# A chunked state-space scan ahead of a gated FFN: every chunk scanned as two halves of 64 tokens on the two halves of the partitions

## The chip, the cores and the metric

The kernel runs on one core of a Trainium2 chip. The metric is the device time of one execution in microseconds, as the median of several runs. A core has five engines that work side by side, each through its own list of instructions in a fixed order: PE (TensorE, matrix products), DVE (VectorE), ACT (ScalarE), POOL (GpSimd) and SP (SyncE, which here only issues DMAs). They wait for one another by semaphores.

## The reference

For each of 4 batches and 8 heads, a sequence of 768 tokens is run through a linear scan with a state of 16 x 32, written in chunks; the result, laid out as 3072 tokens by 256 features, goes through a gated FFN of width 1536. Cut to what matters:

```
for c in range(nc):                                   # chunks of the sequence
    la = log_a[:, :, sl];  cum = np.cumsum(la, axis=-1)
    L = np.exp(cum[..., :, None] - cum[..., None, :]) * causal
    M = np.einsum('bhin,bhjn->bhij', Cc, Bc) * L      # C by B, weighed by decays
    y_intra = np.einsum('bhij,bhjd->bhid', M, xc)     # the product within the chunk
    y_inter = np.einsum('bhin,bhnd->bhid', Cc, state) * np.exp(cum)[..., None]   # the state product
    y[:, :, sl] = y_intra + y_inter
    Bx = np.einsum('bhjn,bhjd->bhjnd', Bc, xc) * decay_from_j[..., None, None]
    state = decay_full[..., None, None] * state + np.sum(Bx, axis=2)
x = y.transpose(0, 2, 1, 3).reshape(batch * seq, heads * head_dim)
out = (sigmoid(x @ w_gate) * (x @ w_val)) @ w_out
```

The length of a chunk is free: any split of the sequence gives the same result.

## The kernel before

The sequence is cut into six chunks of 128 tokens (`L = 128`, `NCH = 6`). One chunk of one batch, with its eight heads, is a *unit*; there are 24, numbered u = 4c + b. The FFN runs once per chunk over the 512 tokens of its four units: 12 blocks f of `gate` and `value` (lines 725 to 766), then four projections `proj` (line 810). Chunk 0's FFN takes plain fp32 weights (line 795, 827); from chunk 1 on, weights and inputs are split in a high and a low fp32r part (lines 804, 837, 838). The split of the weights (`split_w`, `part_w`, lines 305 to 341) runs on ACT, DVE and POOL during chunk 0's FFN and into chunk 1's.

A unit of chunks 1 to 5 does this (class `Unit`, line 357; tile names in brackets as in the profile):

- `products`: B and C are transposed on PE (`pt`, lines 383, 384); ACT copies them and makes two masked copies of C, one for each half of the heads (`bct`, lines 394 to 400).
- `multiply` (line 499): C by B for all tokens of the chunk, four matmuls of 32 rows by 128 columns by 256 (`pcb`, line 506), into four PSUM banks that two units share.
- `decays` (line 412): the decays a are loaded from DRAM (`a_z`), spread over all 128 partitions, and one DVE scan over 8 x 128 elements turns them into all decay products (`ab`, line 418); B is multiplied by the decay to the end of the chunk (line 424).
- `before` (line 429): C times the decay from the start of the chunk (`cd`, line 434), from prefix products loaded from DRAM (`a_p`, tile `pp`).
- `result` (chunk 1, line 436) and `results` (chunks 2 to 5, two units at once, line 516): DVE weighs C by B by the decays (`m`, lines 440 and 524, 8 x 128 columns). Then PE makes the state product, two matmuls of 128 x 128 x 128 with the state masked into a block matrix (`sb`; lines 457 and 536), and into the same bank the product within the chunk, eight matmuls of 128 rows by 32 columns by 144 (lines 463 and 544). The last 16 of the 144 columns give the unit's part of the new state. Then ACT and DVE take the output into the FFN's high and low inputs (`xh`, `xl`), and DVE transposes the state part (lines 480 and 564).
- `state` (line 482): DVE adds the decayed old state (line 486), POOL or DVE makes the block matrix from it (line 494).

Chunk 0 (class `FirstUnit`, line 566) already works in two halves of 64 tokens, the first on partitions 0 to 63 and the second on 64 to 127. Its decays are spread on PE (`pa`, line 585), C by B is made of 32 x 64 tiles (line 605), the product within of 64 x 32 tiles with 80 columns (line 647), the second half's state product from the first half's transposed state (lines 655, 659). There C is permuted on PE (`pc`, line 615), since heads lie in another order on the state's rows.

The order of every engine's list is set ahead by a planner in Python (`run`, line 175). Each piece of work is a task with a due time (`DUES` and `task`, lines 18 and 164) whose steps name an engine, an assumed cost, the keys that must be made before, and the PSUM banks or buffers that they take (`banks` for three general ones, `cb` for the C by B group). The planner always takes the next step that could begin, by due time. SP's DMAs are steps in the same plan; the first nineteen loads have a written order (`FIRST`, line 31).

Of the kernel before, what the change touches and what calls it, by code (L numbers as in the profile page):

```python
# [8 lines left out]
F32 = mybir.dt.float32  # L9
# [31 lines left out]
GV0 = 1.75  # L41
# [22 lines left out]
def tile_ssd_then_gated_ffn(  # L64
# [22 lines left out]
    LB = L + N  # L87
# [3 lines left out]
    NBUF = 3  # L91

    const = ctx.enter_context(tc.tile_pool(name="const", bufs=1))
    ld = ctx.enter_context(tc.tile_pool(name="ld", bufs=NBUF))
# [3 lines left out]
    ps_mm = ctx.enter_context(tc.tile_pool(name="ps_mm", bufs=3, space=PSUM))  # L98
    ps_cb = ctx.enter_context(tc.tile_pool(name="ps_cb", bufs=1, space=PSUM))
    ps_y = ctx.enter_context(tc.tile_pool(name="ps_y", bufs=1, space=PSUM))  # L100
# [12 lines left out]
    for i in range(WARM):  # L113
# [17 lines left out]
    delta2 = hp.tile([P, H, L2], F32, tag="h3", name="delta2")  # L131
    nc.gpsimd.tensor_copy(delta2, eye2.rearrange("p (o l) -> p o l", o=1).broadcast_to([P, H, L2]))
# [13 lines left out]
        of_row.rearrange("p (q g n) -> p q g n", q=NQ, g=NG),  # L146
        head.rearrange("p (g q o) -> p q g o", g=NG, o=1).broadcast_to([NB * H, NQ, NG, N]),
    )

    perm = hp.tile([P, P], F32, tag="h6", name="perm")  # L150
    nc.gpsimd.tensor_copy(
        perm.rearrange("p (q g n) -> p q g n", q=NQ, g=NG), eye.rearrange("p (g q n) -> p q g n", g=NG, q=NQ)
    )
    delta = const.tile([P, H, L], F32, name="delta")
    st = [const.tile([P, D], F32, name=f"st{b}") for b in range(NB)]

    sb = [const.tile([P, NG, NQ, D], F32, name=f"sb{b}") for b in range(NB)]
# [17 lines left out]
    def run():  # L175
# [8 lines left out]
        spare = {"banks": [0.0] * 3, "cb": [0.0], "g": [0.0] * 3, "o": [0.0] * 2}  # L184
# [68 lines left out]
    def load_bc(c, b, n):  # L253
        cs = slice(c * L, (c + 1) * L)
        for tag, src in (("bn", b4), ("cn", c4)):
            t = pair_of(tag, c, b, N)
            if c == 0:
                nc.sync.dma_start(  # L258
                    t[:, b % 2 : b % 2 + n].rearrange("p b h n -> p (b h) n"), src[cs, b * H : (b + n) * H]
                )  # L260
                continue
            for i in range(b, b + n):
                for g in range(NG):
                    nc.sync.dma_start(  # L264
                        t[:, i % 2].rearrange("p (q g) n -> g p q n", g=NG)[g],
                        src[cs, i * H + NQ * g : i * H + NQ * (g + 1)],
                    )
# [6 lines left out]
    def load_a(c, b):  # L274
        u = c * NB + b
        t = ld.tile([P, H, L], F32, tag="ab", name=f"ab{c}_{b}", bufs=NBUF + 1)
        nc.sync.dma_start(t, a_z[b : b + 1, :, c * L : (c + 1) * L].broadcast_to([P, H, L]))
        got["a", u] = t

    def load_p(c, b):  # L280
        t = ld.tile([P, L], F32, tag="pp", name=f"pp{c}_{b}")
# [73 lines left out]
    units = {}  # L355

    class Unit:


        def __init__(self, c, b):  # L360
            self.c, self.b, self.u = c, b, c * NB + b
            self.nm = f"{c}_{b}"
            self.more = c < NCH - 1
            self.w = LB if self.more else L
            self.m = None

        def second(self):

            if self.m is None:
                self.m = wk.tile([P, H, LB], F32, tag="m", name=f"m{self.nm}")  # L370
            return self.m

        def products(self):
# [3 lines left out]
            if c:  # L377
                needs += [("bct", u - 1 if c > 1 else -1), ("cb", u - 2), ("cd", u - 2)]
            needs += [("x", 0, NB - 1)] if c == 1 else []
            yield step("pe", 0.24 if c else 0.45, needs, [("tp", u)], banks=1)  # L380
            bn, cn = (got[k, c, b // 2][:, b % 2].rearrange("p h n -> p (h n)") for k in ("bn", "cn"))
            pt = ps_mm.tile([P, 512], F32, tag="mm", name=f"pt{self.nm}")
            nc.tensor.transpose(pt[:, :L], bn, eye)
            nc.tensor.transpose(pt[:, L : 2 * L], cn, eye)
            yield step("act", 0.9 if c else 1.1, [], [("bct", u)], banks=-1)
            if c:
                self.bct = wk.tile([P, 4, L], F32, tag="bct", name=f"bct{self.nm}")
# [14 lines left out]
            if c == 0:  # L402
                yield step("pe", 0.47, [], [("cb", u)])
                self.multiply()
            elif u == NB:
                yield step("pe", 0.85, [("mult", v) for v in range(NB)], [("cb", u)], cb=1)
                self.multiply()

        def multiply(self):
            multiply(self)  # L410

        def decays(self):

            c, b, u = self.c, self.b, self.u
            yield step("dve", 2.3, [("a", u), ("delta",)], [("scan", u)], port=True)
# [6 lines left out]
            if self.more:  # L422
                yield step("dve", 0.28, [("bc", u), ("scan", u), ("y", u - 2)], [("bdec", u)], port=True)
                nc.vector.tensor_tensor(
                    out=self.second()[:, :, L:], in0=got["bn", c, b // 2][:, b % 2],
                    in1=self.dec[:, :, L - 1 : L].broadcast_to([P, H, N]), op=ALU.mult,
                )

        def before(self):

            c, b, u = self.c, self.b, self.u
            yield step("dve", 0.42, [("bct", u), ("pp", u), ("y", u - 2), ("cd", u - 1 if c > 1 else -1)], [("cd", u)], port=True)
            self.cd = wk.tile([P, L], F32, tag="cd", name=f"cd{self.nm}")
            nc.vector.tensor_tensor(out=self.cd, in0=self.bct[:, 1], in1=got["pp", u], op=ALU.mult)

        def result(self):

            c, b, u = self.c, self.b, self.u
            yield step("dve", 1.22, [("cb", u), ("scan", u), ("y", u - 2)], [("mult", u)], cb=-1)
            nc.vector.tensor_tensor(  # L440
                out=self.second()[:, :, :L].rearrange("p (q g) l -> p q g l", g=NG),
                in0=self.pcb.rearrange("p q (g l) -> p q g l", g=NG),
                in1=self.dec.rearrange("p (q g) l -> p q g l", g=NG), op=ALU.mult,
            )
            needs = [("xn", u), ("lo", u - 1)]
            if self.more:
                needs += [("bdec", u)]
            needs += [("cd", u), ("S", u - NB)]
            then = [u + 1] if b < NB - 1 else [u + 1, u + 2]
            yield step(  # L450
                "pe", 1.25 + 0.65 * len(then), needs + [("bct", v) for v in then], [("y", u)] + [("cb", v) for v in then],
                cb=1,
            )
            xn = got["xn", c, b // 2][:, b % 2]
            py = ps_y.tile([P, NG, LB], F32, tag="py", name=f"py{self.nm}")
            for g in range(NG):
                nc.tensor.matmul(
                    py[:, g, :L], sb[b][:, g].rearrange("p q d -> p (q d)"), self.cd,
                    start=(g == 0), stop=False, skip_group_check=True,
                )  # L460
            for g in range(NG):
                for q in range(NQ):
                    nc.tensor.matmul(
                        py[32 * q : 32 * q + 32, g, : self.w], xn[:, NQ * g + q, :], self.m[:, NG * q + g, : self.w],
                        start=False, stop=True, skip_group_check=True,
                    )
            multiply(*(units[v] for v in then))
            yield step("act", ACT_HALF, [("gv", c - 2)])
            if b == 0:
                xb[c] = [wk.tile([P, NG, 512], F32R, tag=f"x{p}", name=f"x{p}{c}") for p in "hl"]  # L470
            hi = xb[c][0][:, :, b * L : (b + 1) * L]
            nc.scalar.copy(hi, py[:, :, :L])
# [3 lines left out]
            if not self.more:  # L476
                return
# [562 lines left out]
```

## Time and profile before

| | us |
|---|---|
| median of 3 runs | 383.75 |
| lowest and highest | 383.54, 384.74 |
| span of the profiled execution | 382.5 |
| PE busy | 373.1 |
| DVE busy | 205.9 |
| POOL busy | 163.3 |
| ACT busy | 151.2 |

The span goes from the first to the last instruction of one profiled execution; the median is 1.25 us above it. Busy times are those of each engine alone and overlap each other. A group row gives line, engine, operation, output and input names and shapes, count, busy time and the mean of one in ns, then idle time before it and what ended that. A row of the timeline gives start and length in us, engine, line, operation, tiles, shape and count. A row of PE has rows by columns of the tile of the array in use (32*64), then the moving operand (32x128). An fp32 matmul shows as two records. Matmuls are pipelined, so a record's length overlaps the next; the time that a step holds PE is read from start to next start.

### The profile page before, as it was taken

To read this page: it belongs to the slowest core of one execution; us is meant where nothing else is said; L and a number is where in the kernel's file an instruction comes from. 1 tells how busy PE (TensorE), PEld (TensorE's weight loads), DVE (VectorE), ACT (ScalarE), POOL (GpSimd) and SP (SyncE) were. 2 spreads that over 40 slices of the span, in tenths; PEclk is the share of its full clock that TensorE was granted. 3 is DMA by queue.
4 is the path that set the end of the run, shared out by engine and by line. 5 is a ranking of instruction groups with operands and counts; after the bars stand their busy time and mean duration, and the time that the engine had idled before them with its cause. 6 is when DMAs were issued, how large, how long until landed. Compare 5 with 4: busy or idle time off the path is not lost.

```text
span 382.5 us, 5978 instructions
## 1 busy us (share of the span) xinstructions
PE 373.1 (98%) x2264; PEld 286.0 (75%) x2264; DVE 205.9 (54%) x312; ACT 151.2 (40%) x319; POOL 163.3 (43%) x137
## 2 busy tenths in 40 slices
PE   8779999999999999999999999999999999999996
PEld 3445444687788888887788887788887788888885
DVE  4787779887767765225795125785125520122201
ACT  3556456614356631245421246430236430235310
POOL 5353455474289990244471144365044240044410
PEclk9759999999999999999999999999999999999999
DMA  6999686007640635103752003861000000000000
GB/s 82 263 363 367 111 189 168 7 17 143 116 126 3 117 73 134 43 0 44 146 129 69 27 2 36 156 158 40 27 2 7 2 0 29 27 2 0 0 27 29
DMA packets 107461, 31.38 MB, mean 82 GB/s; under 512 B 76554, under 2 KB 102730, under 8 KB 107434
## 3 DMA queue, kind: packets, MB, share of 16 engines
q1 hardware_dynamic: 107434, 31.01, 35.0%
q8 instruction: 18, 0.29, 0.3%
q14 instruction: 9, 0.07, 0.1%
HBM read 27.66 MB, written 3.34 MB: 81 GB/s over the span
## 4 chain that ended last, share of the span: by engine, by line
PE 84%; SPq 8%; DMA 6%; issue 1%; DVE 0%; DVEq 0%
PE pv L804 22%; PE pg L804 22%; PE po L837 14%; PE po L838 7%; PE po L827 6%; PE pcb L506 3%; DMA wr<-in_moe_w_gate_dram 3%; SPq L264 2%; SPq L302 2%; PE py L544 2%; PE py L536 2%; PE pv L795 2%; DMA a<-in_a_dram 2%; SPq L258 1%; PE pg L795 1%; SPq L272 1%
## 5 line engine op out<-in xcount | busy, mean ns | idle before, releaser
L766 POOL TENSOR_TENSOR h<-g,h 128x512 fp32r<-128x512 f32 x60 | 89.6, 1493 | 124.0 <-ACT h L764 123.9
L804 PE MATMUL pg<-xh,w 128*128 128x512 f32 x240 | 85.3, 396 | 0.0
L804 PE MATMUL pv<-xh,w 128*128 128x512 f32 x240 | 84.6, 393 | 0.0
L760 DVE TENSOR_TENSOR g<-pv,g 128x512 f32<-128x512 f32 x60 | 41.3, 689 | 79.4 <-PE pv L804 69.2
L837 PE MATMUL po<-w,h 128*128 128x512 f32 x228 | 81.1, 400 | 0.0
L764 ACT CAST h<-g 128x512 fp32r<-128x512 f32 x60 | 37.3, 621 | 75.9 <-DVE g L760 75.8
L838 PE MATMUL po<-w,h 128*128 128x256 f32 x228 | 64.1, 281 | 0.0
L737 ACT ACTIVATE g<-pg 128x512 f32<-128x512 f32 x72 | 43.0, 598 | 33.3 <-PE pg L804 16.2
L418 DVE TENSOR_TENSOR_SCAN ab<-ab,delta 128x1024 f32<-128x1024 f32 x20 | 50.9, 2551 | 6.2 <-DMA ab<-a_z 6.1
L804 PEld LDWEIGHTS pv<-xh,w 128*128 128x128 f32 x240 | 45.1, 188 | 10.5 <-issue 1.2
L804 PEld LDWEIGHTS pg<-xh,w 128*128 128x128 f32 x240 | 45.1, 188 | 9.7 <-issue 0.5
L837 PEld LDWEIGHTS po<-w,h 128*128 128x128 f32 x228 | 42.9, 188 | 10.9 <-issue 0.4
L804 PE MATMUL pv<-xl,w 128*128 128x512 f32 x120 | 46.8, 390 | 0.0
L804 PE MATMUL pg<-xl,w 128*128 128x512 f32 x120 | 46.8, 390 | 0.0
L838 PEld LDWEIGHTS po<-w,h 128*128 128x128 f32 x228 | 43.1, 189 | 0.3
L852 DVE TENSOR_TENSOR o<-po,o 128x256 f32<-128x256 f32 x20 | 8.5, 424 | 50.8 <-ACT o L850 50.8
L328 POOL TENSOR_TENSOR wr<-wr 128x512 int32<-128x512 int32 x18 | 22.5, 1255 | 29.5 <-ACT wr L326 25.1
L850 ACT COPY o<-po 128x256 f32<-128x256 f32 x20 | 7.4, 372 | 64.1 <-PE po L838 58.0
L341 POOL TENSOR_TENSOR w<-wr,w 128x512 fp32r<-128x512 f32 x18 | 28.8, 1602 | 8.8 <-ACT w L339 6.3
L494 POOL TENSOR_TENSOR sb<-st,of_h 128x256 f32<-128x256 f32 x20 | 14.8, 740 | 31.1 <-DVE st L486 21.1
L804 PEld LDWEIGHTS pv<-xl,w 128*128 128x128 f32 x120 | 22.6, 188 | 4.4
L804 PEld LDWEIGHTS pg<-xl,w 128*128 128x128 f32 x120 | 22.6, 188 | 4.1
(111 smaller groups left out, 433.9 us busy)
## 6 DMA issues: line engine op xcount, KB each, us to landing
ab<-a_z SPq DMA_DIRECT2D x20, 512.0 KB
wr<-in_moe_w_gate_dram SPq DMA_DIRECT2D x6, 512.0 KB
wr<-in_moe_w_val_dram SPq DMA_DIRECT2D x6, 512.0 KB
wr<-in_moe_w_out_dram SPq DMA_DIRECT2D x6, 512.0 KB
out_dram<-o SPq DMA_DIRECT2D x24, 128.0 KB
xn<-in_x_dram SPq DMA_DIRECT2D x10, 256.0 KB
bn<-in_B_dram SPq DMA_DIRECT2D x40, 32.0 KB
cn<-in_C_dram SPq DMA_DIRECT2D x40, 32.0 KB
```

Of the source, the lines that this page charges most:

```text
L328: nc.gpsimd.tensor_tensor(out=lw.bitcast(I32), in0=hw.bitcast(I32), in1=lw.bitcast(I32), op=ALU.add)
L341: engines[eng].tensor_tensor(out=lo, in0=lw, in1=hi.bitcast(F32), op=ALU.subtract)
L418: nc.vector.tensor_tensor_scan(out=t.rearrange("p h l -> p (h l)"), data0=t.rearrange("p h l -> p (h l)"), data1=delta.rearrange("p h l -> ...
L494: engines[eng].tensor_tensor(out=sb[b], in0=st[b].rearrange("p (o r d) -> p o r d", o=1, r=1).broadcast_to([P, NG, NQ, D]), in1=of_h.rearr ...
L737: nc.scalar.activation(gs[k, f], pm, AF.Sigmoid)
L760: nc.vector.tensor_tensor(out=g, in0=pm, in1=g, op=ALU.mult)
L764: copies[eng](hh, g)
L766: engines[eng].tensor_tensor(out=hl, in0=g, in1=hh.bitcast(F32), op=ALU.subtract)
L804: nc.tensor.matmul(pm, w[:, part, kt, fs], xx[:, kt], start=(i == 0), stop=(i == 3 * NK - 1))
L827: nc.tensor.matmul(acc[:, :DM], hs[k, f][:, js], whole[NF + f // 2][:, f % 2], start=(f == 0), stop=(f == NF - 1))
L837: nc.tensor.matmul(acc, hh, w.rearrange("p i m -> p (i m)"), start=(f == 0), stop=False, skip_group_check=True)
L838: nc.tensor.matmul(acc[:, :DM], hl, w[:, 0, :], start=False, stop=(f == NF - 1), skip_group_check=True)
```

## The change

All chunks are scanned as chunk 0 was, in two halves of 64 tokens:

- **Decays.** `a_z` is stored by halves of 64 tokens, and `load_a` brings each half only to its own 64 partitions (512 columns in place of 1024). The scan (`delta`) and the weighing (`weigh`) run over 8 x 64 columns in place of 8 x 128. Six buffers hold decays (`NDEC`), five the prefix products (`NPRE`).
- **C by B.** Eight matmuls of 32 rows by 64 columns by 128 a unit, for chunks 1 to 5 too. Two units lie in the first half of the four banks.
- **Within.** Sixteen matmuls of 64 x 32 by 64 columns, and eight more (four in the last chunk) of the same tile that give each half's part of the new state, two heads at a time. The outputs lie in the second half of the same four banks (columns from 2L on).
- **State.** It is kept as 128 x 64, two heads side by side; a mask on DVE (`chosen`) keeps the right blocks, and two decays on DVE give the state after the first half (`s1`) and after the second (`sn`). The block matrix `sb`, its operation on POOL and the transposes are gone in chunks 1 to 5. The state product is eight matmuls of 32 x 64 by 64 columns a unit, made after the mask and decay of the first half, as a step of its own on PE.
- **Chunk 0.** `pc`, the permutation, the masked prefix products and the transposes are gone; instead DVE makes a wide masked copy of the first half's state part (`wide`), and two matmuls of 128 x 128 by 64 columns use it. The large `delta` is not made any more.
- **Order.** Heads lie in natural order, so B and C are loaded by one DMA each for a pair of units, in place of eight. Chunk 1 is done in pairs too. The transposes of chunks 1 to 5 take `ps_y`'s bank (`y`). The list of due times is another one; in it w0 comes ahead of all B and x, and w2 ahead of w1.

The core of the diff:

```diff
+    NDEC = 6
+    NPRE = 5
...
     def load_a(c, b):
-        t = ld.tile([P, H, L], F32, tag="ab", name=f"ab{c}_{b}", bufs=NBUF + 1)
-        nc.sync.dma_start(t, a_z[b : b + 1, :, c * L : (c + 1) * L].broadcast_to([P, H, L]))
+        t = ld.tile([P, H, L2], F32, tag="ab", name=f"ab{c}_{b}", bufs=NDEC)
+        src = a_z[2 * c : 2 * c + 2, b * H : (b + 1) * H].rearrange("i (o h) l -> i o (h l)", o=1)
+        nc.sync.dma_start(t.rearrange("p h l -> p (h l)"), src.broadcast_to([2, L2, H * L2]))
...
+    def multiply(pcb, at, *us):
+        for k, t in enumerate(us):
+            t.banks = pcb
+            t.pcb = pcb[:, :, (at + k) * L : (at + k + 1) * L]
+            for q in range(NQ):
+                qs = slice(32 * q, 32 * q + 32)
+                for i in range(2):
+                    half = slice(i * L2, (i + 1) * L2)
+                    nc.tensor.matmul(
+                        t.pcb[half, q], t.bct[qs, 0, half], t.bct[qs, 2:4, half], start=True, stop=True
+                    )
...
+    def within(t, out, local, first=True, more=True):
+        xn = got["xn", t.c, t.b // 2][:, t.b % 2]
+        for kt in range(NK):
+            for r in range(NQ):
+                for i in range(2):
+                    half = slice(i * L2, (i + 1) * L2)
+                    nc.tensor.matmul(
+                        out(i, kt, slice(32 * r, 32 * r + 32)), xn[half, NQ * kt + r], t.m[half, NQ * kt + r],
+                        start=first(kt), stop=True, skip_group_check=True,
+                    )
+        for q in range(NQ):
+            for i in range(2 if more else 1):
+                half = slice(i * L2, (i + 1) * L2)
+                nc.tensor.matmul(
+                    local(i, slice(32 * q, 32 * q + 32)), t.bd[half, NG * q : NG * q + NG].rearrange("p g n -> p (g n)"),
+                    xn[half, NG * q : NG * q + NG].rearrange("p g d -> p (g d)"),
+                    start=False, stop=True, skip_group_check=True,
+                )
...
     def results(*two):
...
+        py = two[0].banks[:, :, 2 * L :].rearrange("p (i k) (s u l) -> p i k s u l", i=2, s=2, l=L2)
...
+        yield step("dve", 0.25, [("first", u - 2) for u in us])
+        ml = wk.tile([P, n, NG * D], F32, tag="ml", name=f"ml{two[0].nm}")
+        chosen(ml, py[:, 0, 0, 1], n)
+        for k, (t, u) in enumerate(zip(two, us)):
+            yield step("dve", 0.22, [("S", u - NB), ("pp", u), ("inter", u - NB)], [("first", u)])
+            t.s1 = state_of(u, "sm")
+            nc.vector.scalar_tensor_tensor(
+                out=t.s1, in0=states[u - NB], scalar=t.last(0), in1=ml[:, k], op0=ALU.mult, op1=ALU.add
+            )
+        yield step("pe", 0.2 + 0.23 * n, [("cd", u) for u in us], [("inter", u) for u in us])
+        for k, t in enumerate(two):
+            s0 = states.pop(t.u - NB)
+            for i, state in enumerate((s0, t.s1)):
                 for q in range(NQ):
+                    qs, rows = slice(32 * q, 32 * q + 32), slice(64 * (q % 2), 64 * (q % 2) + 64)
                     nc.tensor.matmul(
+                        py[rows, i, q // 2, 0, k], state[qs], t.cd[qs, i * L2 : (i + 1) * L2],
                         start=False, stop=True, skip_group_check=True,
                     )
...
     class FirstUnit(Unit):
...
+            wide = got["wide"][:, b]
+            local = py[0][:, NK].rearrange("p (o g d) -> p o g d", o=1, g=NG)
             nc.vector.tensor_tensor(
+                out=wide, in0=local.broadcast_to([P, NQ, NG, D]),
+                in1=of_h.rearrange("p (q g o) -> p q g o", g=NG, o=1).broadcast_to([P, NQ, NG, D]), op=ALU.mult,
+            )
...
-        if c < 2:
+        if c == 0:
             task(due, f"result{u.nm}", u.result())
```

More of the change, by code (lines that the diff above doesn't have):

```diff
@@ L145, in tile_ssd_then_gated_ffn @@
     nc.gpsimd.tensor_copy(
[L146 to L157 removed]
+        of_row.rearrange("p (h n) -> p h n", n=N),
+        head.rearrange("p (h o) -> p h o", o=1).broadcast_to([NB * H, H, N]),
+    )
     tasks = []
@@ L363, in __init__ @@
             self.more = c < NCH - 1
[L364 to L371, printed above, removed]
         def products(self):
@@ new lines, in results @@
+            y = py[:, i, :, 0]
+            nc.scalar.copy(hi, y)
+            end = {"cb": -1} if i and not more else {}
+            made = [("x", c, t.b) for t in two] if i else []
+            if i and not more:
+                made += [(k, u) for u in us for k in ("lo", "S", "after")]
+            yield step("dve", DVE_HALF, [], made, **end)
+            nc.vector.tensor_tensor(out=lo, in0=y, in1=hi.bitcast(F32), op=ALU.subtract)
+        if more:
+            yield step("dve", 0.25, [("S", u - 2) for u in us], [(k, u) for u in us for k in ("lo", "after")], cb=-1)
+            ml = wk.tile([P, n, NG * D], F32, tag="mr", name=f"mr{two[0].nm}")
+            chosen(ml, py[:, 1, 0, 1], n)
+            for k, t in enumerate(two):
+                t.after = ml[:, k]
```

397 lines of the change are left out of this document (140 added, 257 removed), and 24 rows, old and new, of the table DUES.

## The prediction

> **What bounds the kernel now.** I read the page's busy line and clock line first, then busy time by stage, then the TensorE timeline around the scan's products, then the groups by shape.
>
> ```profile
> span 382.5 us, 5978 instructions
> PE 373.1 (98%) x2264; PEld 286.0 (75%) x2264; DVE 205.9 (54%) x312; ACT 151.2 (40%) x319; POOL 163.3 (43%) x137
> PEclk9759999999999999999999999999999999999999
> ```
>
> Busy time by stage (start:end, length, then PE, PEld, DVE, ACT, POOL busy, granted clock, DMA share, GB/s):
>
> ```profile
> 24.70:30.73 6.03, 6.03 (x32) 4.38 (x25) 4.03 (x9) 3.23 (x7) 3.29 (x4) 0.66 1.05 385
> 30.73:72.80 42.07, 41.22 (x131) 19.28 (x130) 35.64 (x54) 24.86 (x48) 18.88 (x19) 1.00 0.68 171
> 101.15:155.50 54.35, 54.35 (x334) 45.44 (x333) 35.67 (x49) 24.58 (x49) 39.40 (x29) 1.00 0.45 97
> 329.70:382.50 52.80, 49.59 (x241) 41.59 (x239) 10.84 (x18) 16.48 (x29) 15.46 (x12) 1.00 0.04 16
> ```
>
> PE is the bound: from 30.73 us on it works 41.22 of 42.07 us, then all of 54.35, at clock 1.00; only the tail is idle. The FFN's matmuls are untouched by the change. So two things can move the time: what the scan costs on PE between the FFN's matmuls, and when the FFN starts (24.70). DVE, ACT and POOL have room (35.67, 24.58 and 39.40 of 54.35 in the busiest FFN stage) and count only where PE must wait for them.
>
> **The change, part by part.** *The scan on PE, chunks 2 to 5.* These are PE's rows around one pair of units (start, length as modelled, with a tail that overlaps the next; a step's cost is start to next start).
>
> ```profile
> 176.32 0.39 PE L804 MATMUL pv<-xh,w 128*128 128x512 f32 x1
> 176.64 1.15 PE L506 MATMUL pcb<-bct 32*128 32x256 f32 x16
> 177.71 0.33 PE L383 MATMUL pt<-eye,bn 128*128 128x128 f32 x1
> ...
> 180.77 1.05 PE L536 MATMUL py<-cd,sb 128*128 128x128 f32 x8
> 181.75 1.19 PE L544 MATMUL py<-m,xn 128*32 128x144 f32 x32
> 182.87 0.33 PE L383 MATMUL pt<-eye,bn 128*128 128x128 f32 x1
> ...
> 185.71 0.51 PE L804 MATMUL pv<-xh,w 128*128 128x512 f32 x1
> 186.05 0.40 PE L804 MATMUL pv<-xl,w 128*128 128x512 f32 x1
> 186.29 0.63 PE L804 MATMUL pv<-xh,w 128*128 128x512 f32 x2
> ```
>
> Before, C by B (pcb) costs 1.07 a pair, the state product 0.98, the product within the chunk 1.12. An insertion into the FFN stream also costs about 0.1 at each side: 0.32 from the last pv to pcb and 0.34 between the next two pv, against 0.24 from there to the third.
>
> The new shapes exist already in chunk 0, in smaller numbers: pcb as 32x64 tiles, and the inner product as 64x32 tiles (32 rows from 14.67 to 14.94; four of them and the next step here).
>
> ```profile
> 12.09 0.47 PE L605 MATMUL pcb<-bct 32*64 32x128 f32 x16
> 12.50 0.43 PE L615 MATMUL pc<-bct,perm 128*128 128x64 f32 x2
> 14.67 0.25 PE L647 MATMUL py<-m,xn 64*32 64x80 f32 x1
> ...
> 14.71 0.25 PE L647 MATMUL mm<-m,xn 64*32 64x80 f32 x1
> 14.76 0.23 PE L647 MATMUL py<-m,xn 64*32 64x80 f32 x1
> ...
> 14.94 0.23 PE L647 MATMUL mm<-m,xn 64*32 64x80 f32 x1
> 15.10 0.72 PE L605 MATMUL pcb<-bct 32*64 32x128 f32 x16
> ```
>
> Eight tiles start within 0.04 us, the next eight at 14.76; 32 records take 0.27 from first to last start (8.4 ns each), and 0.16 of drain follows. An fp32 matmul has two records.
> - pcb: one unit took 0.41, that is 0.25 for two rounds of 128 columns and the drain of 0.16. A pair is four rounds: 0.50 + 0.16 = 0.66. Saved: 1.07 - 0.66 = 0.41.
> - Within: 24 matmuls of 64 columns a unit, 48 records, against 32 records of 80 columns in 0.27. By columns 48/32 x 64/80 x 0.27 = 0.32 a unit, by record rate 48/32 x 0.27 = 0.41. A pair with its drain is 0.80 to 0.98; I take 0.90, the middle. Saved: 0.22 (0.14 to 0.32).
> - State product, now 32x64 tiles of 64 columns, no operand masked to 128x128: 16 matmuls a pair, four in flight (q by row group), two records each, so eight rounds of half of 0.125: 0.50 + 0.16 = 0.66. Saved: 0.32. The trace has no such matmul in which two row groups share a column half but not the full set; were only two in flight, 16 rounds make 1.16, a loss of 0.18. I take 0.66, since pcb's row above has four row groups over both halves at once.
> - Within and state product are now two insertions (DVE's masking and decay lie between them): one more, +0.2.
>
> A pair of chunks 2 to 5: results 0.22 + 0.32 - 0.2 = 0.34, eight pairs, 2.7; pcb 0.41, seven pairs, 2.9. Sum 5.6. Transposes stay.
>
> *Chunk 1 goes from single units to pairs.* PE's rows of one unit:
>
> ```profile
> 85.50 0.61 PE L457 MATMUL py<-cd,sb 128*128 128x128 f32 x4
> 86.04 0.70 PE L463 MATMUL py<-m,xn 128*32 128x144 f32 x16
> 86.67 0.71 PE L506 MATMUL pcb<-bct 32*128 32x256 f32 x8
> 87.31 1.85 PE L827 MATMUL po<-wr,h 128*128 128x256 f32 x7
> ```
>
> State 0.54, within 0.63, pcb 0.64 for one unit. Four units: 4 x (0.54 + 0.63) = 4.68, after two pairs of 0.66 + 0.90 = 3.12; saved 1.56. Chunks 1 to 5 hold 20 units; seven pairs of pcb are taken above, six units are left: 4 x 0.64 + 1.07 = 3.63, after three pairs 1.98; saved 1.65. Insertions go from five to seven: +0.4. Sum 2.8.
>
> Together the scan's products save 5.6 + 2.8 = 8.4 us on PE. Ends: 2.4 (within at 0.98, state product at 1.16) and 11.4 (within at 0.80, and the parted steps adjacent to others, so that no insertion is added).
>
> *DVE, ACT, POOL.* DVE's groups in chunks 1 to 5 (first three) and the same work over 64-token rows as chunk 0 has it; the last is POOL's masked state, which goes.
>
> ```profile
> L418 DVE TENSOR_TENSOR_SCAN ab<-ab,delta 128x1024 f32<-128x1024 f32 x20 | 50.9, 2551 | 6.2 <-DMA ab<-a_z 6.1
> L524 DVE TENSOR_TENSOR m<-pcb,ab 128x1024 f32<-128x1024 f32 x16 | 19.1, 1215 | 2.9 <-PE pcb L506 2.9
> L486 DVE SCALAR_TENSOR_TENSOR st<-st,pp,tr 128x32 f32<-128x32 f32 x16 | 6.7, 424 | 0.4
> L591 DVE TENSOR_TENSOR_SCAN ab<-pa,delta 128x512 f32<-128x512 f32 x4 | 4.8, 1217 | 0.6 <-PE pa L585 0.5
> L633 DVE TENSOR_TENSOR m<-pcb,ab 128x512 f32<-128x512 f32 x4 | 2.8, 692 | 2.0 <-PE pcb L605 1.5 <-PE mm L647 0.5
> L494 POOL TENSOR_TENSOR sb<-st,of_h 128x256 f32<-128x256 f32 x20 | 14.8, 740 | 31.1 <-DVE st L486 21.1
> ```
>
> A unit's scan falls from 2.55 to 1.22 and its weighing from 1.22 to 0.69, 1.86 in all; added are one more decay (0.42) and two masks a pair. So 20 units lose over 20 us of DVE, and POOL loses 14.8. None of it is on PE's path, so the term is nothing. What hides it is the FFN, with 0 us of PE idle; it is also the cover for the new order within, mask, decay, state product, in which PE now depends on DVE twice a pair. Where this cover is thin, PE waits. No row shows that wait; I take 0.15 a pair, 1.5 us, with ends 0 and 6. Loads of decays halve and those of B and C become 2 issues in place of 8: SP's queue gets shorter, worth nothing while PE is full.
>
> *One stall goes.* PE stood 0.85 us for an FFN product that stood in DVE's order behind the first scan:
>
> ```profile
> 54.67 3.07 DVE L418 TENSOR_TENSOR_SCAN ab<-ab,delta 128x1024 f32<-128x1024 f32 x1 [0.84 <-DMA ab<-a_z]
> 58.37 0.33 PE L383 MATMUL pt<-eye,bn 128*128 128x128 f32 x1 [0.85 <-DVE h L758]
> ```
>
> With half the scan and half the bytes to wait for I count -0.6; the ends are -0.85 and 0.
>
> *The start.* SP's issue of w1, its landing, the last step of its split, and the first FFN halves:
>
> ```profile
> 12.53 0.58 SPq L298 DMA_DIRECT2D wr<-in_moe_w_val_dram  x1
> 17.38 0.66 ACT L313 ACTIVATE wt<-wr 128x512 f32<-128x512 f32 x1 [1.56 <-DMA wr<-in_moe_w_val_dram]
> 23.64 1.52 POOL L328 TENSOR_TENSOR wr<-wr 128x512 int32<-128x512 int32 x1 [2.06 <-ACT wr L326]
> 24.70 2.07 PE L784 MATMUL pg<-xh,wr 128*128 128x256 f32 x4
> 27.29 1.89 PE L784 MATMUL pv<-xh,wr 128*128 128x256 f32 x4
> ```
>
> The new due times put w0 ahead of all B and x, and w2 ahead of w1. Another 0.5 MB at the 385 GB/s of that stage delays w1 by 1.4; it was whole at 25.2 and used at 27.3, so 2.1 of slack take that. The chunk-0 units lose pc's matmul and its rows, but each puts a wide mask and a state mask on DVE before the next may begin, 0.2 each over the transposes they replace by my estimate: four units, +1.6 as the upper end. The other way, w1 spent 7.8 us from landing to whole on six operations, which make 4.0 if each is as long as the first (0.66); were that queueing gone, -3.8. I take -1.0. The half clock (0.66 in that stage) I leave as it is.
>
> **Sum.** -8.4 - 0.6 - 1.0 + 1.5 = -8.5. The profiled span of 382.5 becomes 374.0. The median of 383.75 is 1.25 above that span, which I take as what lies around it: 375.2.
>
> **The rivals.** (a) *PE waits for DVE in each pair.* After the first product DVE runs a mask and two decays before the state product may go. At 0.42 each (the L486 row, for the mask its upper bound) that is 1.27. If PE's order left nothing between, ten pairs pay 12.7 in place of my 1.5: 375.2 - 1.5 + 12.7 = 386.4, slower. Without any such wait the kernel gains 10.0, so it decides from 1.0 a pair. For it: PE's order is fixed ahead, by costs that are shorter (0.22) than that row. Against: one FFN product (six matmuls at 0.24, 1.4) between covers it, and PE had no idle time in chunks 2 to 5. 0.06.
>
> (b) *Starts of small matmuls set the rate.* A pair has 96 + 32 + 32 = 160 small records, which the sum counts near 8.4 ns. At the L544 row's 35 ns (1.12 over 32) they take 5.6 against 2.2: +3.4 a pair, +34, some 409, slower. It decides from 1.0 a pair, 14.7 ns each. Against it: eight starts in 0.04. 0.03. The Trainium skill, "TensorE: Matmul & The Clock Gate", section "Wait — 56ns, not 53.3ns?", speaks against this change: starts never come closer than about 25 ns, however few the columns. By that, 160 records take 4.0, and my estimate from that page would be about 393. The trace disagrees for tiles: 6 ns between the starts of eight.
>
> (c) *The gain before chunk 1's FFN is eaten.* POOL works 39.40 of 54.35 us there, and splits the weights that this stage needs first. If those set the pace, the 2.8 of chunk 1, the stall's 0.6 and the start's 1.0 are lost: 379.6. Against: POOL loses its masked states, and DVE has time to take over. 0.10, of which 0.03 ends within the measurement's reach.
>
> **How the numbers follow.** The forecast has 0.81, 0.02 of it within 0.3% (about what a measurement here can tell from no change). Faster: 0.79 + 0.07 = 0.86; same: 0.02 + 0.03 = 0.05; slower: (a) and (b), 0.09. The range goes from 370.0 (products at 11.4, the start at -3, no waits: 383.75 - 11.4 - 0.6 - 3 = 368.8, not all at once) to 381.5 (products at 2.4, the rest as taken: 383.75 - 2.4 - 0.6 - 1.0 + 1.5 = 381.3), which takes in (c).
>
> **What would show it.** Right: PE still about 98% busy; pcb near 0.66 a pair, within near 0.9, state product near 0.66; scan and weighing on DVE at 1.2 and 0.7; first FFN half between 21 and 26 us. Wrong: PE idle released by DVE's mask or decay ahead of the state product (a); the products' starts spread to 15 ns or more (b); PE waiting for weight parts from POOL between 95 and 150 us (c); or the FFN's first half well after 26.

## The result, and the profile after

The changed kernel takes 426.42 us (median of 4 runs, 425.40 to 428.30) against 383.99 us for the kernel before on the same chip: a ratio of 1.1112, 95% interval 1.1077 to 1.1146. The forecast was 375.2 us with a range of 370.0 to 381.5. The profiled execution took 427.21 us, with a span of 425.4.

The span, busy time, PE's row in 40 slices, the granted clock and the DMA engines' share, from the page of the kernel after:

```profile
span 425.4 us, 7987 instructions
PE 378.3 (89%) x3312; PEld 287.0 (67%) x3312; DVE 173.3 (41%) x298; ACT 150.4 (35%) x317; POOL 146.8 (35%) x159
PE   8899998036999899881999999999999999999997
PEclk9589999559899899997899999999999999999999
DMA  8999811114572301241702110410000000000001
```

DVE lost 32.6 us of work (205.9 to 173.3), as planned, and POOL 16.5. But PE is at 89% instead of 98%. Its row has holes: a slice of 0 and one of 3 in the eighth and ninth place (74 to 96 us), and a slice of 1 at 191 to 202 us. Under the holes stand clock digits of 5 to 7. The DMA row shows something odder: from 53 to 96 us it reads 1 throughout, neither idle nor busy. The first holes by windows of 10 us (start:end, length, then PE, PEld, DVE, ACT, POOL busy, granted clock, DMA share, GB/s):

```profile
60.00:70.00 10.00, 10.00 (x41) 5.11 (x28) 5.88 (x9) 5.80 (x12) 3.86 (x4) 1.00 0.14 51
70.00:80.00 10.00, 2.73 (x13) 1.92 (x11) 0.00 (x0) 0.00 (x0) 0.00 (x0) 0.82 0.13 49
80.00:90.00 10.00, 0.00 (x0) 0.00 (x0) 1.60 (x2) 0.00 (x0) 0.33 (x1) 0.50 0.10 39
90.00:100.00 10.00, 8.43 (x148) 6.77 (x149) 8.22 (x18) 3.84 (x9) 3.28 (x6) 0.65 0.24 49
```

From 73 to 88 us none of these five engines works, and DMA moves 48 to 49 GB/s on 0.13 of its engines. The forecast's rows show 385 GB/s for the stage before 30 us. A share that stands at 0.13 is what 2 of 16 engines give, and in the trace's DMA packets of these 15 us exactly two are in flight for 92% of the time. The waits say who stands behind it (waiting engine and line, what it waited for: us in total, times, longest):

```profile
DVE ab L409 <- DMA ab<-a_z: 66.2, 13, 21.0
...
PE pcb L480 <- DVE m L468: 18.8, 1, 18.8
```

DVE's scan waited 66.2 us in all for the load of the decays, 21.0 us in one piece, and PE's product within the chunk waited for `m`, the weighed C by B that DVE makes after that scan. Before, the same wait was 6.1 us. The chain that ended last shows the queue itself (start, length, what; the L270 rows are SP's issues of that load):

```profile
53.46 0.51 SPq L270
...
57.78 5.66 SPq L270
...
63.48 5.17 SPq L270
...
68.69 19.65 DMA ab<-a_z
...
88.37 1.24 DVE ab L409
```

The first issue takes 0.51 us, later ones 5.66 and 5.17 us: the queue is full, and an issue goes at the pace at which a load lands. A load is 256 KB (the page's DMA list), and 256 KB at 49 GB/s is 5.3 us. Before, a load of twice the bytes would take 1.4 us at the 385 GB/s above; that is an estimate, no row shows one load alone.

The forecast's own places are in order all the same. PE's first FFN half, and DVE's scan and weighing:

```profile
22.54 2.07 PE L726 MATMUL pg<-xh,wr 128*128 128x256 f32 x4
```

```profile
L409 DVE TENSOR_TENSOR_SCAN ab<-ab,delta 128x512 f32<-128x512 f32 x20 | 25.4, 1278 | 66.2 <-DMA ab<-a_z 66.2
...
L468 DVE TENSOR_TENSOR m<-pcb,ab 128x512 f32<-128x512 f32 x24 | 15.8, 684 | 5.3 <-PE pcb L454 5.1
```

The FFN starts 2.2 us earlier than before (24.70), the scan takes 1.28 us and the weighing 0.68 (1.22 and 0.69 were forecast). In these views only the load is large enough to explain 42 us.

### The profile page after: what moved, and what is told of

The parts are those of the page before. It is cut to its first block, busy times and chain, and to the rows that moved or that the text cites. A ratio compares the mean times of both kernels' runs of the same rounds, so it can differ in the third digit from the quotient of the medians.

```text
span 425.4 us, 7987 instructions
## 1 busy us (share of the span) xinstructions
PE 378.3 (89%) x3312; PEld 287.0 (67%) x3312; DVE 173.3 (41%) x298; ACT 150.4 (35%) x317; POOL 146.8 (35%) x159
## 4 chain that ended last, share of the span: by engine, by line
PE 61%; DMA 26%; SPq 6%; DVE 4%; issue 2%; ACT 1%; DVEq 0%; ACTq 0%
DMA ab<-a_z 18%; PE pv L746 16%; PE pg L746 16%; PE po L779 8%; PE po L780 4%; SPq L270 4%; PE po L769 4%; DMA out_dram<-o 3%; DMA cn<-in_C_dram 3%; PE pg L737 2%; PE pv L737 2%; PE pcb L480 1%; DMA wr<-in_moe_w_gate_dram 1%; DVE m L468 1%; PE pcb L454 1%
## 5 line engine op out<-in xcount | busy, mean ns | idle before, releaser
L708 POOL TENSOR_TENSOR h<-g,h 128x512 fp32r<-128x512 f32 x60 | 77.5, 1291 | 148.7 <-ACT h L706 144.7
L746 PE MATMUL pg<-xh,w 128*128 128x512 f32 x240 | 86.2, 400 | 2.6 <-DVE g L702 2.6
L746 PE MATMUL pv<-xh,w 128*128 128x512 f32 x240 | 87.3, 405 | 0.0
L746 PEld LDWEIGHTS pv<-xh,w 128*128 128x128 f32 x240 | 46.1, 192 | 10.2 <-issue 0.3
L409 DVE TENSOR_TENSOR_SCAN ab<-ab,delta 128x512 f32<-128x512 f32 x20 | 25.4, 1278 | 66.2 <-DMA ab<-a_z 66.2
L746 PE MATMUL pv<-xl,w 128*128 128x512 f32 x120 | 47.7, 398 | 0.0
L321 POOL TENSOR_TENSOR wr<-wr 128x512 int32<-128x512 int32 x18 | 21.0, 1173 | 28.6 <-ACT wr L319 26.8
L334 POOL TENSOR_TENSOR w<-wr,w 128x512 fp32r<-128x512 f32 x18 | 24.2, 1346 | 14.1 <-ACT w L332 11.7
L480 PE MATMUL pcb<-m,xn 64*32 64x64 f32 x640 | 11.0, 241 | 18.8 <-DVE m L468 18.8
L769 PE MATMUL po<-wr,h 128*128 128x256 f32 x96 | 26.6, 430 | 0.0
```

What stands on the lines that cost most here:

```text
L321: nc.gpsimd.tensor_tensor(out=lw.bitcast(I32), in0=hw.bitcast(I32), in1=lw.bitcast(I32), op=ALU.add)
L334: engines[eng].tensor_tensor(out=lo, in0=lw, in1=hi.bitcast(F32), op=ALU.subtract)
L409: nc.vector.tensor_tensor_scan(out=t.rearrange("p h l -> p (h l)"), data0=t.rearrange("p h l -> p (h l)"), data1=delta.rearrange("p h l -> ...
L708: engines[eng].tensor_tensor(out=hl, in0=g, in1=hh.bitcast(F32), op=ALU.subtract)
L746: nc.tensor.matmul(pm, w[:, part, kt, fs], xx[:, kt], start=(i == 0), stop=(i == 3 * NK - 1))
L769: nc.tensor.matmul(acc[:, :DM], hs[k, f][:, js], whole[NF + f // 2][:, f % 2], start=(f == 0), stop=(f == NF - 1))
```

## The experiments

Theory A: the new load's access pattern has the two halves of the chunk as its outermost dimension, of size two, and so only two DMA engines carry it. Rivals: the loads are slow because many partitions read the same source row (B), or for some other reason of the new kernel, its layout or its order (C).

**One load as two.** After, with each decay load issued as two DMAs, one for each half of the partitions. Same bytes, same source rows, same destination.

```diff
-        src = a_z[2 * c : 2 * c + 2, b * H : (b + 1) * H].rearrange("i (o h) l -> i o (h l)", o=1)
-        nc.sync.dma_start(t.rearrange("p h l -> p (h l)"), src.broadcast_to([2, L2, H * L2]))
+        for i in range(2):
+            src = a_z[2 * c + i, b * H : (b + 1) * H].rearrange("(o h) l -> o (h l)", o=1)
+            nc.sync.dma_start(t[i * L2 : (i + 1) * L2].rearrange("p h l -> p (h l)"), src.broadcast_to([L2, H * L2]))
```

> The changed kernel, with each decay load issued as two DMAs, one per half of the partitions (64 partitions by 2 KB each); same bytes, same 2 KB pieces, same source rows, same order of work. Theory A (the shape: with the two halves as outermost dimension a load of 256 KB runs on two of the 16 DMA engines, about 0.13 of them, and takes 5.2 us, so the queue stands and PE with it): DMA share while decays load rises above 0.5, a load takes 1 to 2 us, PE's long idle times go, time 370 to 381 us. Theory B (64 partitions reading one source row is what is slow): the same packets, so no change, 424 to 429 us. Theory C (PE waits on DVE's mask and decay in each pair, and the loads only follow): less than 10 us back, 415 or more.

Measured: 377.37 us (376.75 to 377.92), ratio to before 0.9812 (0.9782 to 0.9842). This one edit takes away 49 us and makes the kernel 1.9% faster than before. Its page:

```profile
span 375.0 us, 8027 instructions
PE 368.3 (98%) x3312; PEld 281.3 (75%) x3312; DVE 174.8 (47%) x298; ACT 150.4 (40%) x317; POOL 149.9 (40%) x159
PEclk9779999999999999999999999999999999999999
DMA  6999943447532055632220052000100000000000
```

The stretch from 70 to 88 us in the kernel after, and then in this one (columns as in the windows above):

```profile
70.00:88.00 18.00, 2.73 (x13) 1.92 (x11) 0.00 (x0) 0.00 (x0) 0.00 (x0) 0.68 0.13 48
```

```profile
70.00:88.00 18.00, 18.00 (x262) 14.16 (x261) 14.47 (x24) 7.14 (x19) 8.11 (x9) 1.00 0.56 94
```

The same stretch is now full: PE 18.00 of 18.00 us, with the DMA at 0.56 of its engines. SP's issues of the first eight loads, in the kernel after (8 DMAs) and in this one (16; start, length), and the scan's wait for the load in this one:

```profile
53.46 38.56 SPq L270 DMA_DIRECT2D ab<-a_z  x8
```

```profile
53.37 17.95 SPq L271 DMA_DIRECT2D ab<-a_z  x16
```

```profile
DVE ab L410 <- DMA ab<-a_z: 1.3, 2, 0.9
```

SP has issued them all after 17.95 us in place of 38.56, and the wait falls from 66.2 to 1.3 us. While most of these loads run, the DMA of this kernel does this:

```profile
56.00:62.00 6.00, 6.00 (x47) 2.90 (x46) 5.07 (x9) 4.53 (x12) 2.59 (x4) 1.00 0.56 203
```

That is 203 GB/s, about four times the 49 of the kernel after, or 1.3 us for a load of 256 KB. The engines are busy for little more than half of it; SP issues one DMA after the other, 0.59 us each by the median, so two of them take 1.2 us, and its issuing now sets the pace. A holds; B and C fall, since source rows, layout and order are those of the kernel after. The comparison also splits the loss. PE's idle time is 425.4 - 378.3 = 47.1 us after and 375.0 - 368.3 = 6.7 here: 40.4 us are waiting. PE's busy time is 378.3 against 368.3 for the same 3312 records: 10.0 us go with the lower clock, 0.939 of full speed on the mean against 0.986. Together 50.4, the whole difference of the spans.

**The same cause put into the kernel before.** The kernel before, with its decays kept twice in DRAM and loaded by one DMA with a leading dimension of two; nothing else of the change.

```diff
-        nc.sync.dma_start(t, a_z[b : b + 1, :, c * L : (c + 1) * L].broadcast_to([P, H, L]))
+        src = a_z[:, c, b * H : (b + 1) * H].rearrange("i (o h) l -> i o (h l)", o=1)
+        nc.sync.dma_start(t.rearrange("p h l -> p (h l)"), src.broadcast_to([2, L2, H * L]))
...
-    a_z = dr.tile([NB, H, S], F32, name="a_z")
+    a_z = dr.tile([2, NCH, NB * H, L], F32, name="a_z")
...
+    def save_z():
+        for i in range(2):
+            nc.sync.dma_start(a_z[i].rearrange("c r l -> r c l"), az.rearrange(chunks, l=L))
```

> The kernel before, with this one thing of the change: decays are kept in two copies in DRAM and a load has a leading dimension of two (one copy for each half of the partitions), pieces of 4 KB; everything else is as before, one more save of 96 KB. Theory A: a load of 512 KB on two engines takes about 10.5 us, four for a chunk 42 us, which nearly fills a pass of the FFN; PE idle beside waits of the scan for its decays, time 405 to 450 us, DMA share near 0.13 there. Theory B and C: the rows are as widely shared as before and PE's order is the old one, 382 to 387 us.

Measured: 533.19 us (531.43 to 535.68), ratio 1.386 (1.3789 to 1.3931). The direction is A's, the size far beyond its 405 to 450. A window and two waits of this kernel:

```profile
66.00:110.00 44.00, 18.54 (x55) 8.18 (x54) 9.99 (x19) 9.66 (x19) 6.26 (x6) 0.66 0.17 55
```

```profile
DVE ab L419 <- DMA ab<-a_z: 84.1, 13, 11.8
...
DVE cd L435 <- DMA pp<-a_p: 51.4, 4, 24.7
```

The expectation counted only waits for the slow load itself, 84.1 us. But other loads stand in the same queue behind it: the decays' products (pp), small ones, were waited for 51.4 us more (5.9 in the control below). A slow load holds up what stands behind it in its queue.

**Its control.** The same two copies in DRAM and the same pieces of 4 KB, with one DMA for each half:

```diff
-        src = a_z[:, c, b * H : (b + 1) * H].rearrange("i (o h) l -> i o (h l)", o=1)
-        nc.sync.dma_start(t.rearrange("p h l -> p (h l)"), src.broadcast_to([2, L2, H * L]))
+        for i in range(2):
+            src = a_z[i, c, b * H : (b + 1) * H].rearrange("(o h) l -> o (h l)", o=1)
+            nc.sync.dma_start(t[i * L2 : (i + 1) * L2].rearrange("p h l -> p (h l)"), src.broadcast_to([L2, H * L]))
```

> The kernel before, with the two copies of decays in DRAM and pieces of 4 KB of the earlier experiment, but one DMA per half of the partitions in place of one DMA with a leading dimension of two. Theory A: the layout, the copies and the piece size cost nothing, the shape did it all: 382 to 388 us. Otherwise (the layout or the 4 KB pieces are slow): 450 us or more.

Measured: 385.34 us (384.88 to 385.79), ratio 1.0027 (1.0004 to 1.0049). So layout, second copy and size of the pieces cost together 0.3%, and 148 us of the experiment above come from the leading dimension alone.

**A divisor, or a count?** Is it enough that the outermost size is 16 or more, or must 16 divide it? The first experiment's loads, cut again into 62 and 2 partitions of each half:

```diff
-            nc.sync.dma_start(t[i * L2 : (i + 1) * L2].rearrange("p h l -> p (h l)"), src.broadcast_to([L2, H * L2]))
+            for p0, p1 in ((0, 62), (62, 64)):
+                nc.sync.dma_start(
+                    t[i * L2 + p0 : i * L2 + p1].rearrange("p h l -> p (h l)"), src.broadcast_to([p1 - p0, H * L2])
+                )
```

> The changed kernel, with four DMAs per decay load: in each half 62 partitions and 2 partitions. Same bytes and pieces. The Trainium skill (DMA: Bandwidth & Descriptors, section on why a DMA increments its semaphore by 16) says that a DMA takes the largest number of engines up to 16 that divides its outermost size: 62 then goes on 2 engines, a load takes about 5 us as in the changed kernel, 415 to 430 us, DMA share near 0.13 while PE waits. Rival (any outermost size of 16 or more takes all 16 engines): 376 to 380 us, as with 64.

Measured: 427.43 us (426.27 to 429.23), ratio 1.1139 (1.1104 to 1.1174), the time of the kernel after again. The same stretch of this kernel:

```profile
70.00:88.00 18.00, 2.88 (x13) 2.07 (x11) 0.00 (x0) 0.00 (x0) 0.00 (x0) 0.64 0.13 49
```

62 is 2 times 31, and the share is 0.13 again: it is the divisor that counts. The prediction did not weigh the rule that says this: the Trainium skill, "DMA: Bandwidth & Descriptors", section "Why a DMA increments its semaphore by 16 and not by 1", says that a DMA uses the largest number of engines, up to 16, that divides the outermost sizes of both patterns. The runs agree, at 0.13 for 2 and for 62, and 0.56 with 64. In its section "Rules for kernel authors" a row says the same of an outermost dimension of a few copies: it confines the DMA to as many engines. Another row there advises one transfer over 128 partitions in place of two over disjoint halves; here the kernel with one took 426.42 us and the kernel with two 377.37, since the one, as it is written, has the two halves outermost.

**Does every chunk pay, or only the first?** Two DMAs for chunk 1 alone, which has to fill an empty pipeline:

```diff
+        if c == 1:
+            for i in range(2):
+                src = a_z[2 * c + i, b * H : (b + 1) * H].rearrange("(o h) l -> o (h l)", o=1)
+                nc.sync.dma_start(t[i * L2 : (i + 1) * L2].rearrange("p h l -> p (h l)"), src.broadcast_to([L2, H * L2]))
+        else:
+            src = a_z[2 * c : 2 * c + 2, b * H : (b + 1) * H].rearrange("i (o h) l -> i o (h l)", o=1)
+            nc.sync.dma_start(t.rearrange("p h l -> p (h l)"), src.broadcast_to([2, L2, H * L2]))
```

> The changed kernel, with two DMAs only for the decay loads of chunk 1, one DMA over both halves for chunks 2 to 5. Theory A: a load on two engines takes 5.2 us, four for a chunk 21 us of a pass of about 55; where loads of chunk 2 stand ahead of chunk 1's in SP's order they still delay it. If the loss is that of filling once (22 us of idle PE between 70 and 92 us), 395 to 405 us; if the shape costs again in every chunk as long as loads queue, 405 to 420. Theory B or C: 424 to 429.

Measured: 410.82 us (409.30 to 411.64), ratio 1.0697 (1.0665 to 1.0730), in the second of theory A's ranges. Two windows of this kernel:

```profile
80.00:90.00 10.00, 4.39 (x48) 3.04 (x46) 7.30 (x12) 1.46 (x3) 2.67 (x3) 0.89 0.33 58
170.00:180.00 10.00, 5.54 (x31) 4.52 (x29) 1.22 (x1) 0.00 (x0) 0.00 (x0) 1.00 0.28 74
```

PE is still half idle at 80 to 90 us and again at 170 to 180. Mending chunk 1 alone gives back 426.4 - 410.8 = 15.6 us, and mending the later chunks as well another 410.8 - 377.4 = 33.4: the cost comes back.

**What is left of the forecast: the product within the chunk.** With the load mended, the terms of the forecast can be measured one by one (below); one was off, the pair's product within the chunk, at 1.12 us where 0.90 was forecast. Theories on it were tried in two runs. S says that PE loses time where its two kinds of product alternate, R that the state parts are slow in themselves. All output parts of a pair first, then all state parts:

```diff
-        for k, t in enumerate(two):
-            within(
-                t, lambda i, kt, rows: py[rows, i, kt, 0, k], lambda i, rows: py[rows, i, 0, 1, k], lambda kt: k == 0, more
-            )
+        for part in range(2):
+            for k, t in enumerate(two):
+                within(
+                    t, lambda i, kt, rows: py[rows, i, kt, 0, k], lambda i, rows: py[rows, i, 0, 1, k],
+                    lambda kt: k == 0, more, (part,),
+                )
```

> The first experiment's kernel (two DMAs per decay load), with the product within the chunk in another order: for a pair of units first the 2 x 16 matmuls of the outputs, then the 2 x 8 of the state parts, where it was 16, 8, 16, 8. In the first experiment this step took 1.12 us a pair, where 0.90 was forecast: 32 records of the outputs in 0.26, but 16 of the state parts in 0.24. Theory S (going from one kind to the other and back costs about 0.1 each time): the step falls to about 0.95, the kernel by 10 x 0.2 = 2 us, to 375 to 376. Theory R (state parts are slow in themselves, 15 ns a record): 1.12 stays, 377 to 378.

Measured: 379.0 us (377.82 to 381.49), ratio 0.988 (0.9848 to 0.9913), 1 us above the range of R and further from that of S. PE's rows of the step:

```profile
215.17 0.80 PE L481 MATMUL pcb<-m,xn 64*32 64x64 f32 x60
215.75 0.24 PE L488 MATMUL pcb<-xn,bd 64*32 64x64 f32 x1
...
215.83 0.51 PE L488 MATMUL pcb<-xn,bd 64*32 64x64 f32 x30
216.27 0.33 PE L375 MATMUL pt<-eye,bn 128*128 128x128 f32 x1
```

The step took 1.10 us (215.17 to 216.27), so S falls. R falls by the same rows: the first 60 records, all of outputs, take 0.58 us to the first state part, 9.7 ns each, and the last 30, all state parts, 0.44 us to the next step, which is 9 ns each without the drain of 0.16. State parts are no slower than outputs. Next, in chunks 1 to 5, half the columns of the output products; this leaves out half of that product's result.

```diff
+        cut = L2 // 2 if t.c else L2
...
-                        out(i, kt, slice(32 * r, 32 * r + 32)), xn[half, NQ * kt + r], t.m[half, NQ * kt + r],
+                        out(i, kt, slice(32 * r, 32 * r + 32))[:, :cut], xn[half, NQ * kt + r], t.m[half, NQ * kt + r, :cut],
...
-                        start=False, stop=True, skip_group_check=True,
+                        start=True, stop=True, skip_group_check=True,
```

> The first experiment's kernel, with half of the work left out in one place: in chunks 1 to 5 the 16 matmuls per unit that give the outputs within the chunk move 32 columns in place of 64, and the state product overwrites their result. The number of matmuls stays. Theory N (the columns set this step's time): the 64 records of the outputs take half, and the step falls from 1.12 to about 0.85 us a pair; the kernel gets about 2.5 us shorter, 374 to 375.5. Theory Q (the rate at which PE can be fed such small matmuls sets it, about 10 ns a record over a burst of 96): the step stays at 1.05 to 1.12, the kernel within 1 us, 376 to 378.

Measured: 377.6 us (375.83 to 378.72), ratio 0.9845 (0.9803 to 0.9886). PE's rows of the step in this kernel (start, length, line, shapes):

```profile
213.69 0.36 PE L482 MATMUL pcb<-m,xn 64*32 64x32 f32 x32
...
214.77 0.33 PE L375 MATMUL pt<-eye,bn 128*128 128x128 f32 x1
```

1.08 us with half the columns in two thirds of the records, against 1.12: N falls, the columns of the outputs do not set this step. What is left is Q, a time per record whatever its columns, some 10 ns over 96 records ((1.12 - 0.16 of drain) / 96). Whether the matmul or the weight load that goes with each record sets it, no run here separates.

**The order of the first loads.** The first experiment's kernel without the new due times of the early loads:

```diff
-    "ap": -143.9, "b0": -890.9, "x0": -647.8, "b1": -735.7, "b2": -249.4, "x2": -91.9, "w0": -1118.8, "w2": -303.1,
+    "ap": -143.9,
```

> The first experiment's kernel without the seven due times that put w0 ahead of B and x and w2 ahead of w1; the loads of the start then go in the written order, as in the kernel before. In the first experiment the first FFN half began at 21.3 us against 24.7 before, and the second block of the FFN at 28.5 against 30.7. Theory D (the order of the loads brought that): the first half begins at 23.5 to 25.5, time 379 to 381. Theory E (the shorter work of chunk 0 on PE, POOL and ACT brought it, and the order does not matter): it begins at 20.5 to 22, time 376 to 378.

Measured: 397.41 us (396.41 to 398.14), ratio 1.0364 (1.0325 to 1.0403), outside what either theory expected. The first FFN half comes at 23.26 us, the second only at 28.15, and PE has new idle time as late as 40 to 50 us:

```profile
40.00:50.00 10.00, 6.72 (x17) 2.79 (x16) 6.52 (x13) 5.98 (x12) 3.97 (x4) 0.98 0.90 105
```

In this run PE waits 2.6 us for weights that POOL splits, which it does nowhere in the first experiment. The planner places every later step by what came before, so taking out seven due times probably moved more than seven loads; no run here separates that. The run says what the seven due times are worth together in this plan, and not what the early loads are worth by themselves.

**How far does the start vary?** The first experiment's kernel once more:

> The first experiment's kernel again, beside the two others on the same chip and with more rounds, as the version that beats both: 376 to 379 us, ratio to the kernel before 0.978 to 0.986.

Measured: 377.71 us (377.57 to 379.17), ratio 0.986 (0.9823 to 0.9898). PE's first row of the FFN's second block in this execution, and in the first one of the same kernel:

```profile
30.41 1.88 PE L738 MATMUL pg<-xh,wr 128*128 128x512 f32 x4
```

```profile
28.49 1.88 PE L738 MATMUL pg<-xh,wr 128*128 128x512 f32 x4
```

The same program differs by 1.9 us in its start between two executions. Before it was 30.73, after 29.72: differences of the size forecast for the start can't be read from one profile each.

## Why the prediction was wrong

The step that failed is the last sentence on DVE, ACT and POOL: "Loads of decays halve and those of B and C become 2 issues in place of 8: SP's queue gets shorter, worth nothing while PE is full." The loads were costed by bytes and number. Their pattern, `[2, L2, H * L2]` with two as its outermost size, stood in the diff and was not costed at all. By the runs it makes a load of 5.3 us out of one that takes 1.3 us in the first experiment, and twenty of these in one queue cost 49 us. (The kernel's own plan counts 0.95 us for the transfer, line 870 of the kernel after.) The cover named for it, a full PE, is no cover: eight of these loads were issued between 53 and 92 us, and PE's products depend on each through DVE's scan. None of the rivals had a transfer in it, nor did any of the signs listed as what would show the forecast wrong.

The other steps, measured where the load is mended. PE's rows of one pair in the first experiment:

```profile
214.31 0.45 PE L481 MATMUL pcb<-m,xn 64*32 64x64 f32 x32
...
215.43 0.33 PE L375 MATMUL pt<-eye,bn 128*128 128x128 f32 x1
...
218.57 0.34 PE L532 MATMUL pcb<-cd,sn 32*64 32x64 f32 x8
...
219.20 0.33 PE L375 MATMUL pt<-eye,bn 128*128 128x128 f32 x1
```

```profile
223.94 0.69 PE L455 MATMUL pcb<-bct 32*64 32x128 f32 x32
224.56 0.50 PE L747 MATMUL pg<-xh,w 128*128 128x512 f32 x1
```

- *PE is the bound.* Right with the load mended (98%), wrong for the change as it was made (89%).
- *C by B.* Forecast 0.66 a pair, measured 0.62 (223.94 to 224.56). Right.
- *State product.* Forecast 0.66, measured 0.63 (218.57 to 219.20). Right: the time is that of four row groups side by side, and the bound of 1.16 falls.
- *Within the chunk.* Forecast 0.90, measured 1.12 (214.31 to 215.43), no gain over before. The term was scaled from a burst of 32 records at 8.4 ns; a run of 96 holds only some 10 ns. The forecast's own upper end, 0.98, did not hold it. This term was mis-sized, and it is a small one.
- *Sum of the products.* With these three: C by B 0.45 x 7 = 3.15; results (0.35 + 0 - 0.2) x 8 = 1.2; chunk 1 0.90 + 0.28 + 1.77 - 0.4 = 2.55. That is 6.9 in place of 8.4, inside the ends of 2.4 and 11.4. (By its own terms the lower end comes to 2.6: 8.4 - 10 x 0.08 - 10 x 0.50.)
- *The stall.* Gone: PE works 10.00 of the 10 us from 50 to 60 in the first experiment.
- *The start.* Forecast -1.0; the second FFN block is 2.2 earlier in one execution of the mended kernel and 0.3 in the other. No contradiction, and no proof.
- *Waits for DVE*, 1.5 forecast. One wait in the mended kernel, of 0.56 us (PE's list of waits, then the window):

```profile
PE pcb L532 <- DVE sm L523: 0.6, 1, 0.6
```

```profile
130.00:140.00 10.00, 9.44 (x165) 7.62 (x164) 6.76 (x11) 4.67 (x9) 8.29 (x8) 1.00 0.53 114
```

The mended kernel's 377.37 lies 2.2 above the forecast. Its span is 7.5 below that of before (whose profiled execution was probably the slowest of its three: other executions of that kernel lie 2.3 to 2.4 us above their spans, not 1.25); -6.9 - 0.85 + 0.56 and the start's -2.2 make -9.4. Of the 1.9 us between them the insertions hold about 0.8: from 28.8 us on, PE's rows show the FFN's stream broken in 43 places in the first experiment and in 29 before, 14 more where the sum has ten. Against the median spacing of unbroken FFN matmuls the matmuls at the breaks take 6.4 us longer, before 3.5; that is +2.8 where the sum has +2.0. The other 1.1 us stays open. The gain itself is known no better than to 2 us: by medians on the same chip it is 7.1 us in the first experiment and 5.2 in the last.

*The rivals.* (a) PE waiting for DVE in each pair: seen once, at 0.56, against the 1.0 a pair from which it decides. (b) The rate of small records: the mechanism is there in one of three products, but at some 10 ns and not at the 14.7 from which it decides. By the 25 ns of the Trainium skill, "TensorE: Matmul & The Clock Gate", section "Wait — 56ns, not 53.3ns?", 96 records would take 2.4 us; the trace has 1.12. (c) POOL's pace: no wait for weights appears in the mended kernel between 95 and 150 us.

## What to carry to other kernels

Cost a load by three things, its bytes, its pieces and the outermost size of both its patterns: here sizes of 2 and 62 kept a load to 0.13 of the engines, and two DMAs of 64 partitions each moved about four times as much in the same time (203 against 49 GB/s). In a profile this shows as a DMA share that stands still at a fraction such as 0.13 while an engine waits for a load. A load that is "hidden" stays so only while the whole queue keeps up, for what stands behind it in the same queue waits as well.

## What the runs showed of the hardware

- Two engines carry 48 to 49 GB/s at a share of 0.13, and 62 partitions get no more than 2 do.
- A stall is paid twice. The clock falls to 0.50 while PE stands still and is at 0.65 in the next 10 us; the first pair's product after the long stall began like this in the kernel after (start, length; in brackets the idle time and its releaser):

```profile
91.57 0.68 PE L480 MATMUL pcb<-m,xn 64*32 64x64 f32 x32 [18.84 <-DVE m L468]
...
93.15 2.07 PE L769 MATMUL po<-wr,h 128*128 128x256 f32 x4
```

It took 1.58 us against 1.12 at full clock. Over the whole kernel PE's busy time is 10.0 us longer than in the first experiment, of 50.4 us lost, at a mean clock of 0.939 against 0.986.
- Records of small 64x32 tiles start about 8 ns apart for the first 32 (0.26 us, 214.31 to 214.57) and about 11 ns apart for the 64 behind them (0.70 us to 215.43, without the drain of 0.16). With 32 columns in place of 64 in two thirds of them the step still takes 1.08 us in place of 1.12.
